# Gated linear attention and a gated projection on one core: scores and values with swapped rows in every second pair, weights in two channel orders, fewer zero products, and a new order of the program

## The chip, the cores and the metric

The kernel runs on one core of a Trainium2 chip. The time is in device microseconds (us), for one execution of the program. The engines are PE (TensorE: matrix products, with PEld for its weight loads), DVE (VectorE), ACT (ScalarE), POOL (GpSimd) and SP (SyncE, which starts the DMAs here). "Clock" is TensorE's granted clock as a share of full speed.

## The reference

```python
f = 1 / (1 + exp(-f_logit))            # B, H, S, D = 4, 8, 768, 48; all float32
for t in range(S):
    state = f[:, :, t, :, None] * state + k[:, :, t, :, None] * v[:, :, t, None, :]
    y[:, :, t] = einsum('bhd,bhde->bhe', q[:, :, t], state)
x = y.transpose(0, 2, 1, 3).reshape(B, S, H * D)           # 4, 768, 384
gate_pre = sum(conv_w[k] * xp[:, k:k + S] for k in range(5))  # causal, per channel
out = (sigmoid(gate_pre) * (x @ w_val)) @ w_out
```

## The kernel before, in words

**Tiles.** The sequence is cut into six blocks `c` of 128 steps. The eight heads go in four pairs `p`; a pair's two heads `s` lie on rows 0 to 47 and 64 to 111 of q, k and the decays. Batches go two by two in halves `h`. Of a block's 128 steps the first 64 and the last 64 are told apart (`u`), since a step looks only at earlier ones.

**Steps of a block.** `csum` (PE, with the triangle `below`; blocks 0 and 1) or `scan` (DVE; blocks 2 to 5) sums the logs of the decays; `pexp`, `pln`, `exp1`, `exp2` on ACT make decays of them; `pmulk` and `pmulq` (DVE) multiply them into k and q. `ktrans` and `kevac` turn k over, `dstate` (PE), `stend` (DVE) and `stmul` (POOL) carry the state `st` from block to block. `scores c b` makes k^T q of a batch on PE, in the four quadrants of 64 rows by 64 columns: per pair two products of 128 columns and two of 64. `mask` (DVE) and `cross` (ACT) bring them to `asb`. `apply c h` makes y^T on PE from the state (part 0) and from `asb` and v (part 1), in columns of 32: head 0's first 32 channels and head 1's are made in two row halves at once ("half height"), the other products with all rows ("full height"). `xevac` (ACT) copies y to `XF`.

**Projections.** `msplit` (ACT) and `mlow` (DVE) split y into a high and a low part. `conv` makes the five taps on PE with diagonal matrices for the blocks in `CONV` (0, 1 and the two halves 5 and 6 of the last block); for blocks 2 to 4 they are made on DVE (`mlast`, `mconv`, 12 per block). `gate` is the sigmoid on ACT, `mval` the product with w_val (nine products of 512 columns for one of three channel groups `m`, 256 columns for a half of the last block), `mmul`, `mhigh`, `mrest` multiply and split again, `mout` is the product with w_out, `mstore` and `out` write it. The conv on PE leaves channel groups in another order of rows (`TURN`) than DVE does, so the gates of blocks 2 to 4 are written in pieces (`MOVES`: 1, 2 and 4 activations for the three groups). The weights come as float64 and are turned into float32 on the chip in `weight` steps (POOL, ACT, DVE).

**Order.** `PROGRAM` is a string of some 500 steps written out in order; `Ordered` chains PE, DVE and ACT to exactly that order. POOL and SP (DMA starts) are ordered by the scheduler from the same string. PSUM is three `pairs` of two banks (`pair`, `done`) and two single banks `mps` (`take`, `give`). `busy n` puts n products with zeros (128x512, bf16) into the bank that the next `pair` or `take` hands out, before its own use. Every fp32 product is two records on PE. Where a decay is out of range a flag sends the program to a general path, which is not run here.

Of the kernel before, what the change touches and what calls it, by code (L numbers as in the profile page):

```python
# [52 lines left out]
ktrans 0 0; exp1 0 1; pmulq 0 1; wload 0; weight 0; weight 0; weight 0; weight 0; pmulq 0 0; busy 3; scores 0 1;
weight 0; mask 0 1; weight 0; weight 0; loadf 1 0; pexp 1 0; loadk 0 2; loadw 0 0; kevac 0 0; dstate 0 0; stend 0 0;
scores 0 0; mask 0 0; pln 1 0; cross 0 1; csum 1 0; exp2 0 2; exp1 0 2; wload 1; pmulk 0 2; ktrans 0 1; cross 0 0;
csum 1 1; okc 0; loadq 0 2; pmulq 0 2; weight 1; weight 1; weight 1; weight 1; weight 1; weight 1; exp2 1 0; loadv 0
0; kevac 0 1; loadw 0 1; dstate 0 1; exp1 1 0; loadv 0 1; apply 0 0 1; stend 0 1; scores 0 3; exp2 1 1; exp1 1 1;
loadk 1 0; pmulk 1 0; ktrans 1 0; weight 1; xevac 0 0; scores 0 2; kevac 1 0; loadk 1 1; pmulk 1 1; ktrans 1 1; weight
2; mask 0 3; cross 0 3; loadq 1 0; pmulq 1 0; busy 2; scores 1 0; weight 2; weight 2; weight 1; weight 3; weight 3;
kevac 1 1; apply 1 0 0; mask 0 2; cross 0 2; scores 1 1; mask 1 0; cross 1 0; loadf 2 0; pexp 2 0; loadv 0 2; apply 0  # L60
1 1; xevac 0 1; weight 2; weight 3; okc 1; weight 2; weight 3; weight 2; weight 3; mask 1 1; cross 1 1; loadq 1 1;
pmulq 1 1; pln 2 0; weight 3; weight 2; loadw 1 0; dstate 1 0; stend 1 0; scores 1 2; mask 1 2; cross 1 2; msplit 0;
scan 2 0; exp2 2 0; exp1 2 0; loadw 1 1; dstate 1 1; stend 1 1; scores 1 3; loadv 1 0; apply 1 0 1; halo 1; xevac 1 0;
conv 0; apply 1 1 0; scan 2 1; exp2 2 1; mask 1 3; weight 3; cross 1 3; mlow 0; wload 2; loadk 2 0; loadk 2 1; pmulk 2
1; ktrans 2 1; loadv 1 1; apply 1 1 1; weight 2; weight 4; stmul 1 1; stmul 1 0; weight 3; mval 0 1; weight 5; weight
4; weight 4; exp1 2 1; okc 2; weight 4; gate 0 0; kevac 2 1; weight 4; weight 4; weight 4; pmulk 2 0; ktrans 2 0;
loadq 2 0; pmulq 2 0; gate 0 1; loadw 2 1; dstate 2 1; weight 5; weight 5; weight 5; gate 0 2; xevac 1 1; mmul 0 1;
# [724 lines left out]
```

## Time and profile before

| | us |
|---|---|
| median of 3 runs (219.23 to 220.79) | 219.87 |
| profiled execution, span from first to last instruction | 217.0 |
| median of the runs above that span | 2.87 |
| PE busy | 196.5 (91%) |
| DVE busy | 147.7 (68%) |
| ACT busy | 140.1 (65%) |

The trace is of one execution. It gives its span; the times of the runs also hold what lies around the span, so a sum over rows is to be compared with 217.0 and not with 219.87. "Busy" is the time in which at least one instruction of the engine runs. PE's count holds products with zeros too.

### The profile page before, as it was taken

The page shows a single profiled execution, that of the slowest core. Times are in us where ns is not written, and L with a number is a line of the kernel's source. Part 1 is how long each engine was busy: PE and PEld are TensorE (multiplying, and loading weights), DVE is VectorE, ACT ScalarE, POOL GpSimd, SP SyncE. Part 2 cuts the span into 40 slices and gives each one's busy share as a digit, 9 for nine tenths or more (in the row PEclk, how much of TensorE's full clock was granted, in tenths as well). Part 3 has the DMA queues.
Part 4 walks back from the last instruction along what each step waited for, and adds up shares of the span by engine and source line. Part 5 has one row for each costly group of instructions (what it writes and reads, how often), then busy time and mean ns, then how long its engine had stood idle before and what let it go on. Part 6 is the DMA issues. An engine that isn't in the chain of part 4 may idle for free.

```text
span 217.0 us, 8352 instructions
## 1 busy us (share of the span) xinstructions
PE 196.5 (91%) x3776; PEld 151.1 (70%) x3778; DVE 147.7 (68%) x200; ACT 140.1 (65%) x220; POOL 33.4 (15%) x43
## 2 busy tenths in 40 slices
PE   3999897939998999999999999999999997989960
PEld 1457786728667876688878878887887885867850
DVE  6005588734999899968789897999686629185000
ACT  4507894436986969778667898787976553645120
POOL 4001205006866323000400002100000000000000
PEclk9999999966999999999999999999999999999996
DMA  6999999977288669262498424012000004100321
GB/s 212 366 377 417 420 425 421 416 276 221 101 316 313 180 239 386 89 189 99 135 309 320 180 91 144 3 51 101 3 5 3 3 0 159 41 0 0 110 108 39
DMA packets 11562, 39.42 MB, mean 182 GB/s; under 512 B 1408, under 2 KB 2304, under 8 KB 10752
## 3 DMA queue, kind: packets, MB, share of 16 engines
q1 hardware_dynamic: 11520, 38.82, 48.8%
q8 instruction: 31, 0.51, 1.0%
q14 instruction: 11, 0.09, 0.1%
HBM read 34.09 MB, written 4.72 MB: 179 GB/s over the span
## 4 chain that ended last, share of the span: by engine, by line
PE 87%; DVE 3%; issue 3%; ACT 2%; DMA 1%; DVEq 0%; ACTq 0%
PE pair L119 60%; PE mps L119 27%; DMA out<-osb 1%; ACT osb L119 1%; DVE keep L119 0%; DVE pair L119 0%; ACT xf L119 0%; DVE e L119 0%; DVE kb L119 0%; ACT qb L119 0%; DVE asb L119 0%; DVE st L119 0%; DVE pre L119 0%; DVE gt L119 0%; ACT e L119 0%
## 5 line engine op out<-in xcount | busy, mean ns | idle before, releaser
L119 ACT ACTIVATE e<-e 112x1024 f32<-112x1024 f32 (+4 forms) x32 | 39.7, 1247 | 4.2 <-DMA e<-in_ft 1.9
L119 PE MATMUL pair<-asb,vb 128*32 128x64 f32 (+2 forms) x1152 | 24.4, 252 | 4.4 <-issue 4.4
L119 DVE SCALAR_TENSOR_TENSOR pre<-xf,cws,pre 128x512 f32<-128x512 f32 x36 | 26.2, 746 | 0.3
L119 PE MATMUL pair<-qb,kb 48*64 48x64 f32 (+1 forms) x768 | 25.0, 260 | 1.3 <-DVE st L119 0.9
L119 PEld LDWEIGHTS pair<-asb,vb 128*32 128x32 f32 (+1 forms) x1152 | 19.5, 111 | 9.2 <-issue 8.5
L119 DVE TENSOR_TENSOR kb<-kb,e 112x1024 f32<-112x1024 f32 (+1 forms) x13 | 16.4, 1272 | 12.9 <-ACT e L119 12.9
L119 DVE TENSOR_TENSOR asb<-pair,tri 128x512 f32<-128x512 f32 x24 | 16.4, 686 | 12.5 <-PE pair L119 12.5
L119 PEld LDWEIGHTS pair<-qb,kb 48*64 48x64 f32 x768 | 21.3, 136 | 4.6 <-DVE st L119 1.0
L119 DVE TENSOR_TENSOR_SCAN e<-keep,e 112x1024 f32<-112x1024 bf16 x8 | 19.1, 2385 | 1.3 <-issue 1.3
L119 PE MATMUL mps<-rg,woH 128*128 128x512 f32 x60 | 19.1, 398 | 0.0
L119 PE MATMUL pair<-idle 128*128 128x512 bf16 x52 | 14.3, 428 | 3.7 <-DVE pair L119 3.6
L119 ACT COPY xf<-pair 128x512 f32<-128x512 f32 (+1 forms) x24 | 10.3, 483 | 11.1 <-PE pair L119 11.1
L119 PE MATMUL mps<-xH,wvH 128*128 128x512 f32 x39 | 16.4, 421 | 0.0
L119 PE MATMUL mps<-xf,WD 32*32 32x256 f32 (+1 forms) x200 | 16.3, 465 | 0.0
L119 ACT ACTIVATE e<-pair 112x1024 f32<-112x1024 f32 (+2 forms) x13 | 9.2, 750 | 11.0 <-PE pair L119 11.0
L119 PE MATMUL pair<-xf,WD 32*32 32x512 f32 (+1 forms) x280 | 15.6, 501 | 0.0
L119 DVE TENSOR_TENSOR qb<-qb,e 112x1024 f32<-112x1024 f32 (+1 forms) x13 | 15.5, 1196 | 0.0
L119 PE MATMUL mps<-xL,wvH 128*128 128x512 f32 x39 | 15.4, 395 | 0.0
L119 PE MATMUL mps<-xH,wvL 128*128 128x512 f32 x39 | 15.4, 395 | 0.0
L119 PE MATMUL pair<-rg,woH 128*128 128x512 f32 (+1 forms) x48 | 12.8, 355 | 2.0 <-ACT osb L119 2.0
L119 ACT COPY asb<-pair 128x256 f32<-128x256 f32 x24 | 8.6, 374 | 8.3 <-DVE asb L119 8.1
L368 POOL TENSOR_TENSOR st<-st,e 112x512 f32<-112x512 f32 x8 | 11.0, 1379 | 17.6 <-ACT ksb L119 9.1
(103 smaller groups left out, 379.8 us busy)
## 6 DMA issues: line engine op xcount, KB each, us to landing
vb<-in_v SPq DMA_DIRECT2D x11, 640.0 KB, 5.9
kb<-in_k SPq DMA_DIRECT2D x11, 512.0 KB, 6.8
qb<-in_q SPq DMA_DIRECT2D x11, 512.0 KB, 7.1
vs<-in_vn SPq DMA_DIRECT2D x10, 512.0 KB, 5.0
e<-in_f SPq DMA_DIRECT2D x4, 1024.0 KB, 6.7
out<-osb SPq DMA_DIRECT2D x15, 256.0 KB, 2.3
raww<-in_wv SPq DMA_DIRECT2D x1, 1152.0 KB, 10.6
raww<-in_wo SPq DMA_DIRECT2D x1, 1152.0 KB, 13.4
```

Of the source, the lines that this page charges most:

```text
L119: ins = emit(*a, **kw)
L368: nc.gpsimd.tensor_tensor(out=s, in0=s, in1=decay(c, h), op=ALU.mult)
```

## The change

- `scores`: odd pairs write their heads to the other row half; pairs 0 and 1 come together, then 2 and 3, first the 128-wide products of both, then the 64-wide ones. The bank is now the pair's parity.
- `apply` has four parts: 0 (state, half height), 1 (state, full height), 2 (values, full height) and 3 (values, half height). v is laid out in 128 columns in place of 160, with both 64-step halves next to each other, and odd pairs with heads swapped.
- `xevac` is one copy in place of two; `gate` of blocks 2 to 4 one activation of 1536 elements in place of seven; two conv banks go in one gate.
- w_val and w_out come in the channel order of the conv on PE (`wvT`, `woT`); the order for blocks 2 to 4 is made from it by `wturn`: two copies on POOL and four DMAs within SBUF (0.79 MB). Weights are loaded in thirds.
- `dstate` takes one bank (`mps`) in place of a pair; four `asb` buffers in place of three; PSUM is one tile `banks`.
- `busy` runs 8 products in all, over the eight banks, in place of 52 (44 ahead of the first `csum`); the three DVE clears of rows 32 to 63 are gone.
- POOL and SP are chained to the program's order too, and `PROGRAM` is written anew.

```diff
-VA, VB = 64, 96
+VA, VB = 64, 64
-MOVES = [[(0, 0, 128)], [(0, 64, 64), (64, 0, 64)], [(r * 32, (r ^ 1) * 32, 32) for r in range(4)]]
+WVB, WVT = 160, 512
+AT = [0, 2 * WVB, WVB]
+LEAD = [0, 64, 32]
 PROGRAM = """
-loadf 0 0; halo 0; pexp 0 0; pln 0 0; busy 44; csum 0 0; loadf 0 1; pexp 0 1; pexp 0 2; pln 0 1; busy 4; csum 0 1; pln
...
+halo 0; loadf 0 0; pexp 0 0; pln 0 0; busy 8; csum 0 0; loadf 0 1; loadv 0 0; loadq 0 0; loadf 1 0; wload 3; loadk 0
...
     PE, DVE, ACT = Ordered(tc, nc.tensor), Ordered(tc, nc.vector), Ordered(tc, nc.scalar)
+    POOL, SP = Ordered(tc, nc.gpsimd), Ordered(tc, nc.sync)
...
-    NA = 3
+    NA = 4
...
     def busy(n):
-        todo[0] = n
...
+        for i in range(n):
+            PE.matmul(banks[:, i % 8], keep[:, 0], keep[:, 0:4], start=True, stop=True)
...
-    for t in pairs:
-        DVE.memset(t[32:64], 0.0)
...
+    def wturn(n):
+        if n == 0:
+            for m in (1, 2):
+                at, k = AT[m], LEAD[m]
+                POOL.tensor_copy(wvT[:, :, :, at + 128 : at + 128 + k], wvT[:, :, :, at : at + k])
+        else:
+            k = LEAD[n]
+            SP.dma_start(woN[: 128 - k, :, n - 1].bitcast(F32), woT[k:, :, n].bitcast(F32))
+            SP.dma_start(woN[128 - k :, :, n - 1].bitcast(F32), woT[:k, :, n].bitcast(F32))
...
     def dstate(c, h):
-        t, ks = pair("d", c, h), KSB[slot(c, h)]
+        t, ks = take("d", c, h), KSB[slot(c, h)]
...
     def scores(c, b):
-        for p in range(NP):
+        for p0 in range(0, NP, 2):
             for u in range(2):
-                for s in range(2):
-                    at = HC * (s ^ u)
-                    PE.matmul(t[at : at + HC, u, p * C : p * C + C - u * HC], kt[rows(s), b * NP + p, u * HC : u * HC + HC],
-                              qt[rows(s), b * NP + p, u * HC :], start=True, stop=True, tile_position=(s * 64, at))
+                for p in (p0, p0 + 1):
+                    for s in range(2):
+                        at, o = HC * (s ^ p & 1), (2 * u + p // 2) * C
+                        PE.matmul(t[at : at + HC, p & 1, o : o + C - u * HC],
+                                  kt[rows(s), b * NP + p, u * HC : u * HC + HC], qt[rows(s), b * NP + p, u * HC :],
+                                  start=True, stop=True, tile_position=(s * 64, at))
...
     def apply(c, h, n):
...
+                    if n == 1:
+                        PE.matmul(to(b, 1, 0, z), st[:, bp, 0:32], qt[:112, bp], start=False, stop=False,
+                                  tile_position=(0, z * 32))
+                    elif n == 2:
+                        PE.matmul(to(b, 1, u, z), vt[:, bp, VA * u : VA * u + 32], at_[:, aat(z, u)],
+                                  start=False, stop=end and c == 0, tile_position=(0, z * 32))
...
+                        for s in range(2):
+                            x = s ^ (z & 1) if n else s
+                            r = slice(x * HC, x * HC + HC)
+                            lhs, rhs = ((vt[r, bp, VA * u + 32 : VA * u + 64], at_[r, aat(z, u)]) if n else
+                                        (st[rows(s), bp, 32:64], qt[rows(s), bp]))
...
-    def mgate(w, m):
+    def mgate(w):
+        act(SIG, w["gt"], w["pre"], AF.Sigmoid)
```

PE at the start. The rows before are the end of the 44 zero products' row and what follows the first `csum` products (`below` is the triangle, `e1` the logs, `ident` the matrix of `ktrans`).

```order
L119 MATMUL pair1_102<-below_72,e10_81 112x128 x4
L119 MATMUL pair2_103<-below_72,e10_81 112x128 x8
L119 LDWEIGHTS idle_80
L119 MATMUL pair0_101<-idle_80 128x512
L119 MATMUL pair0_101<-ident_79,kb0_66 128x112 x8
```

The same place after the change, from the last of the eight zero products on.

```order
L121 MATMUL banks_101<-keep_71 128x512
L121 MATMUL banks_101<-below_72,e10_80 112x128 x16
L121 MATMUL banks_101<-ident_79,kb0_66 128x112 x8
L121 MATMUL banks_101<-below_72,e11_81 112x128 x16
L121 MATMUL banks_101<-ident_79,kb0_66 128x112 x8
L121 MATMUL banks_101<-vs_70,ksb0_87 48x64 x16
L121 MATMUL banks_101<-qb0_64,kb0_66 64x128 x4
```

No zero product stands between the steps any more, and `csum` of block 1 (`e11`) and both `ktrans` of block 0 come ahead of the first scores.

PE in block 2, before: the last pairs of a `scores` (`qb0,kb0`), and the values' part of an `apply` (`asb,vb0`; two batches).

```order
L119 MATMUL pair1_102<-qb0_64,kb0_66 64x128 x2
L119 MATMUL pair1_102<-qb0_64,kb0_66 64x64 x2
L119 MATMUL pair2_103<-asb2_86,vb0_68 32x128 x8
L119 MATMUL pair2_103<-asb0_84,vb0_68 32x128 x8
L119 MATMUL pair2_103<-asb2_86,vb0_68 32x128 x4
L119 MATMUL pair2_103<-asb2_86,vb0_68 32x64 x12
L119 MATMUL pair2_103<-asb0_84,vb0_68 32x128 x4
L119 MATMUL pair2_103<-asb0_84,vb0_68 32x64 x12
```

The same place after: the last pairs of a `scores`, then parts 1, 2 and 3 of an `apply`.

```order
L121 MATMUL banks_101<-qb0_64,kb0_66 64x128 x4
L121 MATMUL banks_101<-qb0_64,kb0_66 64x64 x4
L121 MATMUL banks_101<-qb0_64,st0_74 32x128 x8
L121 MATMUL banks_101<-asb2_85,vb0_68 32x128 x4
L121 MATMUL banks_101<-asb2_85,vb0_68 32x64 x4
L121 MATMUL banks_101<-asb3_86,vb0_68 32x128 x4
L121 MATMUL banks_101<-asb3_86,vb0_68 32x64 x4
L121 MATMUL banks_101<-asb2_85,vb0_68 32x128 x8
L121 MATMUL banks_101<-asb2_85,vb0_68 32x64 x8
L121 MATMUL banks_101<-asb3_86,vb0_68 32x128 x8
L121 MATMUL banks_101<-asb3_86,vb0_68 32x64 x8
```

Of the 64-column products eight a batch are now in the half-height part, and four in the full-height part where twelve stood.

SP's loads, before, from the second load of logs (`in_ft`; `in_vn` is v for `dstate`, `in_wv` w_val).

```order
L645 DMA e11_82<-in_ft 128x1792
L645 DMA kb0_66<-in_k 128x1024
L645 DMA vs_70<-in_vn 128x1024
L221 DMA raww0_94<-in_wv 128x2304
L645 DMA qb0_64<-in_q 128x1024
L645 DMA vb0_68<-in_v 128x640
```

After, from the load that follows the first logs.

```order
L121 DMA vb0_68<-in_v 128x512
L121 DMA qb0_64<-in_q 128x512
L121 DMA e11_81<-in_ft 128x1792
L121 DMA raww0_94<-in_wv 128x768
L121 DMA kb0_66<-in_k 128x512
L121 DMA rawcw_99<-in_cw 128x30
```

The first v, which stood behind the logs of block 1 and all of w_val, now stands ahead of both.

## Rows read from the trace of the kernel before

**Rows 1.** The page, part 1 (busy time, share of the span, instructions of each engine), and from part 2 what the DMA engines moved in 40 equal slices of 5.425 us, in GB/s.

```profile
PE 196.5 (91%) x3776; PEld 151.1 (70%) x3778; DVE 147.7 (68%) x200; ACT 140.1 (65%) x220; POOL 33.4 (15%) x43
GB/s 212 366 377 417 420 425 421 416 276 221 101 316 313 180 239 386 89 189 99 135 309 320 180 91 144 3 51 101 3 5 3 3 0 159 41 0 0 110 108 39
```

**Rows 2.** Busy time of each engine by stretch. Columns: stretch and its length in us, busy us (and instructions) of PE, PEld, DVE, ACT, POOL, granted clock of PE, busy share of the DMA engines (above 1 where transfers overlap), GB/s. 56.78 is the start of block 0's conv on PE, 210.33 the end of the last projection product, 164.70 to 167.43 the conv of a half block.

```profile
0.00:3.65 3.65, 0.00 (x1) 0.10 (x1) 2.19 (x5) 1.39 (x2) 2.42 (x16) 1.00 0.46 135
3.65:15.20 11.55, 11.55 (x44) 4.91 (x44) 1.82 (x2) 4.05 (x9) 0.20 (x1) 1.00 1.02 370
15.20:56.78 41.58, 35.51 (x826) 29.56 (x826) 26.19 (x41) 26.60 (x39) 10.34 (x10) 0.92 0.92 361
56.78:210.33 153.55, 149.30 (x2915) 116.50 (x2908) 117.36 (x152) 107.69 (x170) 20.46 (x17) 1.00 0.36 125
210.33:217.00 6.67, 0.12 (x2) 0.01 (x2) 0.15 (x1) 0.37 (x1) 0.00 (x0) 0.68 0.21 71
60.00:90.00 30.00, 29.19 (x741) 20.63 (x718) 29.04 (x34) 24.32 (x34) 12.70 (x9) 1.00 0.73 261
164.70:167.43 2.73, 2.73 (x122) 2.03 (x121) 2.16 (x3) 1.04 (x2) 0.00 (x0) 1.00 0.02 6
180.00:210.33 30.33, 26.90 (x259) 21.88 (x257) 13.10 (x21) 12.33 (x25) 0.00 (x0) 1.00 0.17 62
```

**Rows 3.** The order in time at the start, PE's rows and two of ACT's. Columns: start in us, us, engine, operation, out<-in, count, and in brackets idle time before it and what ended that.

```profile
3.65 11.77 PE L119 MATMUL pair<-idle 128*128 128x512 bf16 x44 [3.65 <-DVE pair L119]
...
4.25 0.58 ACT L119 ACTIVATE e<-e 128x448 f32<-128x448 f32 x1
...
15.25 1.04 PE L119 MATMUL pair<-below,e 128*112 128x128 f32 x8
...
16.99 2.78 PE L119 MATMUL pair<-below,e 128*112 128x128 f32 x24
```

**Rows 4.** The longest wait of PE in the first 60 us and the stretch behind it, columns as in rows 2.

```profile
43.70:46.20 2.50, 0.02 (x1) 0.00 (x0) 0.00 (x0) 1.03 (x2) 0.00 (x0) 0.86 1.00 379
46.20:52.80 6.60, 5.60 (x118) 5.02 (x120) 3.01 (x5) 3.34 (x5) 1.83 (x3) 0.54 0.65 204
```

**Rows 5.** PE's waits over the span: what was waited for, us in total, times, the longest. "issue" is a wait for which the profile shows no releaser.

```profile
PE pair L119 <- issue: 4.4, 3, 2.5
PE pair L119 <- DVE pair L119: 3.6, 1, 3.6
```

**Rows 6.** PE's order in time from 106 to 116 us: four groups of scores, one `mval`, an `apply` (state, then, after a `ktrans`, values), and the start of a `mout`.

```profile
106.01 3.71 PE L119 MATMUL pair<-qb,kb 48*64 48x128 f32 x128
109.65 0.50 PE L119 MATMUL mps<-xH,wvH 128*128 128x512 f32 x1
...
111.94 1.24 PE L119 MATMUL pair<-qb,st 48*32 48x128 f32 x48
113.11 0.98 PE L119 MATMUL pair<-ident,kb 112*128 112x112 f32 x8
114.03 1.91 PE L119 MATMUL pair<-asb,vb 64*32 64x128 f32 x96
115.87 0.50 PE L119 MATMUL mps<-rg,woH 128*128 128x512 f32 x1
```

**Rows 7.** The values' part of that `apply` in two pieces, columns as in rows 2: half height (both batches), then the full-height part of the first batch.

```profile
114.00:114.60 0.60, 0.60 (x34) 0.40 (x32) 0.60 (x2) 0.57 (x2) 0.00 (x0) 1.00 1.00 396
114.60:115.20 0.60, 0.60 (x40) 0.57 (x36) 0.60 (x2) 0.60 (x1) 0.00 (x0) 1.00 0.92 382
```

**Rows 8.** DVE's instructions in groups by operation and shape. Columns: count, busy us in all, mean ns of one, idle time before them and what ended it.

```profile
L119 DVE SCALAR_TENSOR_TENSOR pre<-xf,cws,pre 128x512 f32<-128x512 f32 x36 | 26.2, 746 | 0.3
L119 DVE TENSOR_TENSOR_SCAN e<-keep,e 112x1024 f32<-112x1024 bf16 x8 | 19.1, 2385 | 1.3 <-issue 1.3
L119 DVE TENSOR_TENSOR asb<-pair,tri 128x512 f32<-128x512 f32 x24 | 16.4, 686 | 12.5 <-PE pair L119 12.5
L119 DVE TENSOR_TENSOR kb<-kb,e 112x1024 f32<-112x1024 f32 x11 | 15.1, 1378 | 0.0
L119 DVE TENSOR_TENSOR qb<-qb,e 112x1024 f32<-112x1024 f32 x11 | 14.2, 1289 | 0.0
L119 DVE TENSOR_TENSOR rg<-gt,rg 128x512 fp32r<-128x512 f32 x15 | 9.9, 683 | 2.1 <-ACT rg L119 2.0
L119 DVE TENSOR_TENSOR xL<-xf,xH 128x1536 fp32r<-128x1536 f32 x5 | 9.0, 1794 | 0.0
L119 DVE TENSOR_TENSOR st<-st,pair 112x512 f32<-112x512 f32 x8 | 5.4, 682 | 4.5 <-PE pair L119 2.8 <-ACT e L119 1.7
L119 DVE SCALAR_TENSOR_TENSOR work<-raww,work 128x384 int32<-128x384 int32 x6 | 4.1, 677 | 0.1
L119 DVE SCALAR_TENSOR_TENSOR work<-work 128x384 int32<-128x384 int32 x6 | 3.3, 550 | 0.1
L119 DVE TENSOR_SCALAR work<-work 128x384 int32<-128x384 int32 x6 | 2.3, 389 | 0.1
```

**Rows 9.** The sigmoids that read `pre` (blocks 2 to 4): count, duration in ns (least, median, most), first and last start in us, shapes.

```profile
L119 ACT ACTIVATE gt<-pre x21: 625/629/634, 127.2 to 196.0; 32x512 f32<-32x512 f32 x12, 64x512 f32<-64x512 f32 x6, 128x512 f32<-128x512 f32 x3
```

**Rows 10.** PE's last products: the end of a group of nine half-width products, and the flag's product behind it.

```profile
209.11 0.40 PE L119 MATMUL pair<-rvb,woH 128*128 128x256 f32 x2
...
210.26 0.19 PE L119 MATMUL mps<-ones,cnt 128*1 128x1 f32 x2
```

More of the change, by code (lines that the diff above doesn't have):

```diff
@@ L53 @@
[L53 to L67, printed above, removed]
@@ L73 @@
-3; pmulk 3 0; mrest 0 0; mrest 0 1; mmul 0 2; mlow 1; pln 4 0; scan 4 0; loadk 4 0; loadk 3 1; exp2 3 1; pmulk 3 1;
-conv 1; apply 2 1 0; ktrans 3 0; kevac 3 0; apply 2 1 1; mval 1 1; loadk 4 1; loadq 3 0; loadw 3 0; dstate 3 0; gate 1
-0; gate 1 1; mmul 1 1; ktrans 3 1; mhigh 0 2; mrest 0 2; xevac 2 1; weight 5; weight 6; halo 3; gate 1 2; scan 4 1;
-mval 1 2; mmul 1 2; exp1 3 1; pmulq 3 1; mlast 2 0; mconv 2 0 0; exp1 3 0; mout 0 2; mstore 0 2; exp2 4 0; mout 0 0;
-mstore 0 0; kevac 3 1; pmulq 3 0; pmulk 4 0; mout 0 1; mhigh 1 2; loadv 4 1; loadq 4 1; loadq 4 0; loadv 4 0; out 0 2;
@@ L78 @@
-dstate 3 1; scores 3 2; stend 3 0; mconv 2 0 1; scores 3 3; stend 3 1; stmul 3 1; mstore 0 1; mhigh 1 1; mask 3 2;
-cross 3 2; mrest 1 1; mlast 2 1; scores 3 0; mask 3 0; scores 3 1; mask 3 1; cross 3 1; mrest 1 2; okc 3; cross 3 0;
-mlast 2 2; exp1 4 0; mval 1 0; mconv 2 1 0; mmul 1 0; mconv 2 1 1; mhigh 1 0; mrest 1 0; apply 3 0 0; out 0 0; ktrans
-4 0; loadv 3 0; apply 3 0 1; mconv 2 2 0; mconv 2 0 2; mconv 2 2 1; mask 3 3; mconv 2 2 2; out 0 1; exp2 4 1; pmulk 4
-1; exp1 4 1; msplit 2; mlow 2; stmul 3 0; loadf 5 0; cross 3 3; mout 1 0; mstore 1 0; xevac 3 0; loadw 4 0; loadk 5 0;
@@ L83 @@
-out 1 0; mconv 2 1 2; mout 1 2; mstore 1 2; mout 1 1; pexp 5 0; mval 2 0; mstore 1 1; mconv 2 0 3; mconv 2 1 3; mconv
-2 2 3; pmulq 4 0; pln 5 0; scan 5 1; kevac 4 0; gate 2 0; gate 2 1; pmulq 4 1; scan 5 0; mval 2 1; mmul 2 1; apply 3 1
-0; ktrans 4 1; loadw 4 1; out 1 2; loadv 3 1; apply 3 1 1; scores 4 1; kevac 4 1; dstate 4 1; xevac 3 1; gate 2 2;
-mhigh 2 1; mlast 3 2; mask 4 1; dstate 4 0; stend 4 0; stend 4 1; mval 2 2; mmul 2 0; mhigh 2 0; okc 4; mmul 2 2;
-cross 4 1; scores 4 0; mask 4 0; cross 4 0; scores 4 2; scores 4 3; mconv 3 2 0; mrest 2 1; mhigh 2 2; mrest 2 2;
@@ new lines @@
+1; conv 1; okc 2; scan 3 1; mask 2 1; weight 5; cross 2 1; mhigh 0 2; msplit 1; exp2 3 1; weight 6; mrest 0 2; mlow 1;
+exp1 3 1; scan 3 0; pmulq 3 1; pmulk 3 1; apply 2 0 1; apply 2 0 2; apply 2 0 3; mval 1 1; gate 1 1; mval 1 0; xevac 2
+0; mlast 2 0; gate 1 0; mlast 2 2; stmul 2 0; weight 6; weight 5; stmul 2 1; halo 2; halo 3; wturn 0; mmul 1 1; mconv
+2 0 0; mconv 2 2 0; mout 0 0; mmul 1 0; mval 1 2; exp2 3 0; exp1 3 0; loadw 3 0; loadq 3 0; pmulk 3 0; pmulq 3 0;
+apply 3 0 0; scores 3 1; loadv 4 0; loadf 4 0; loadv 4 1; loadk 4 0; loadv 3 1; mstore 0 0; out 0 0; loadq 4 0; loadw
@@ new lines @@
+3 1; loadv 3 0; loadq 4 1; loadk 4 1; mlast 2 1; scores 3 0; mconv 2 2 1; mconv 2 0 1; mconv 2 1 0; mout 0 1; mconv 2
+0 2; mmul 1 2; mconv 2 2 2; mout 0 2; msplit 2; pexp 4 0; mask 3 0; mconv 2 1 1; mask 3 1; cross 3 1; ktrans 3 0; pln
+4 0; cross 3 0; ktrans 3 1; mstore 0 1; kevac 3 1; apply 3 0 1; apply 3 0 2; apply 3 0 3; apply 3 1 0; mstore 0 2;
+dstate 3 1; mhigh 1 1; kevac 3 0; dstate 3 0; xevac 3 0; scores 3 2; scores 3 3; scan 4 0; mconv 2 2 3; scan 4 1; mlow
+2; stend 3 0; stend 3 1; mconv 2 1 2; mask 3 3; mconv 2 1 3; mhigh 1 2; mrest 1 2; mask 3 2; exp2 4 1; exp1 4 1; mhigh
@@ L659, in out_ @@
         buf, dst = bufs[n, m]
-        (nc.scalar if engine else nc.sync).dma_start(dst, buf)
+        (ACT if engine else SP).dma_start(dst, buf)
     def mul(n, m):
```

264 lines of the change are left out of this document (139 added, 125 removed).

## The prediction

> **What bounds the kernel now.** I read the page's first part first: PE is busy for 91% of the span, DVE for 68%, ACT for 65% [rows 1]. A kernel at 91% of one engine can gain in only two ways, less work on PE or less time in which PE does something useless or stands, so the second look is at stages [rows 2]. Until 3.65 us PE has nothing. From 3.65 to 15.20 us it is "busy" for 11.55 us with 44 products, and these are the zero products of the step `busy`, queued ahead of the first `csum` [rows 3]: not work. From 15.20 to 56.78 us, where the conv of block 0 starts, it is busy for 35.51 of 41.58 us at a mean clock of 0.92. From there to the last projection product at 210.33 us it is busy for 149.30 of 153.55 us; 6.67 us follow in which only the last store and the flag check run. In the dense middle DVE is as full as PE: 29.04 of 30 us between 60 and 90 us, PE 29.19. After 180 us DVE has 13.1 us of 30, and PE is alone at 26.9. So there are three stages with three limits: A, the start (loads, and what PE waits for); B, up to the last `apply` (PE and DVE together); C, the projections at the end (PE alone).
>
> The profiled execution is the span, 217.0 us, and what the measured time holds around it; the median of the runs, 219.87 us, lies 2.87 us above the span. I sum the span and add 2.87.
>
> **PE work that the change removes.** Scores: four groups take 3.71 us, less the overlap of the last record 3.64, so 0.91 each [rows 6]. Each group has 32 records on four quadrants of the array. Before, two quadrants carry all eight 128-wide ones and the other two the eight 64-wide ones, and 0.91 / 8 = 0.114 us is one 128-wide record on its quadrant (the 24 records of `csum`, each alone on the array, take 2.78 / 24 = 0.116 [rows 3]). A 64-wide one I take from `apply`, whose last batch, 0.58 us of full-height products, holds 2 records of 128 and 6 of 64 columns: (0.58 - 0.23) / 6 = 0.059 [rows 7]. With swapped rows in every second pair each quadrant carries four of either kind: 4 x 0.114 + 4 x 0.059 = 0.69. That is 0.22 less, 5.3 us for 24 groups.
>
> Apply: a half now takes 1.17 us for the state and 1.84 for the values (111.94 to 113.11, 114.03 to 115.87 [rows 6]). The values are 4 x 0.116 of half height, then 4 x 0.116 and 12 x 0.059 of full height, 1.63, and some 0.2 of turning between heights. After: two pieces of 4 x 0.116 + 4 x 0.059 each, 1.40, and one turn less (about 0.15, my reading of the 0.24 that the state's piece has above its eight records). So 0.37 less for each of ten halves, and 0.26 for the two of block 0, which have no state: 4.2 us. Together 9.5 us.
>
> Here a rule of the notes speaks against the change. The trace shows row halves working side by side: both heads of a pair sit on different rows and write one bank in the same group, and that group takes 0.91 us, where its sixteen 128-wide records one after another would take 16 x 0.116 = 1.86 [rows 3, 6]. The Trainium skill, "TensorEngine Tiling (Array Packing)", Gotcha 1: PSUM Pressure, says that different row tiles cannot access the same PSUM bank at once. By that rule the new half-height piece and the swapped scores would run in series; the trace disagrees for partitions that differ, which is how the new pieces write too. I give it a rival below.
>
> **ACT, DVE, POOL.** The gates of blocks 2 to 4 are 21 activations of 0.63 us, 13.2 us [rows 9]; three of 1536 elements replace them. ACT is not full (65%), so this is worth nothing by itself: it unloads the end of B and C. One `xevac` copy for two, one gate for two banks: also ACT only. The three clears of pair rows leave DVE's first 6 us; PE's start waited for the first (3.6 us [rows 5]), but then only zero products began. The two POOL copies and 0.79 MB of weight moves run where POOL has 20 us of 153 and DMA 36% [rows 2]: nothing. `dstate` in one bank instead of a pair and a fourth buffer for the masked scores change no duration; they let PE run further ahead, and I count nothing for that. The zero products, strict order on POOL and SP, and the new program's order are what stage A and the rivals turn on.
>
> **Stage A, to the start of block 0's conv: before 56.78.**
> - Logs ready at 4.25 + 0.58 = 4.83, csum at 15.25, behind 44 zero products [rows 3]. With 8 zero products it starts at about 4.9: -10.4.
> - Three waits of PE for late loads, 4.4 us, the longest of them 2.5 [rows 5], fall if the new load order is right: PE reaches them earlier, but v now comes before f and k of later blocks, in a smaller tile. -4.4.
> - During that longest wait (43.7 to 46.2 us) the granted clock fell to a mean of 0.86, from 46.2 to 52.8 its mean was 0.54, so nearly all of it on the lower of its two levels (1.2 of 2.4 GHz) [rows 4]. 6.6 us at 0.54 cost 6.6 x 0.46 = 3.0. Without the wait they go: -3.0.
> - Six score groups and two applies cheaper: 6 x 0.22 + 2 x 0.26 = -1.8.
> - Two score groups and most of `apply 1 0` stand behind the conv now: -4.3. They are paid in B.
>
> 56.78 - 23.9 = 32.9. This is a lower price, since it has every wait gone. The floor by transfer: in the new order 10.35 MB stand ahead of all that the conv needs of block 1, which the first five slices of the page's rate row (5.425 us each, 9.7 MB) and 1.5 us of the sixth would bring by 28.7 us [rows 1]; then `dstate`, the rest of `apply` and two score groups, 2.4 us: 31. I take 36, which is 32.9 and 3 for waits that a start 10 us nearer to its loads will find, and for a spell at half clock such as [rows 4] shows; bounds 33 (the sum and nothing more) and 42 (the load waits, 4.4, and the half-clock spell, 3, with some 2 for a second one).
>
> The Trainium skill, "TensorE: Matmul & The Clock Gate", HAM oscillation, says that waits for loads between groups of products throw TensorE's clock back to half again and again. By it, 44 zero products dropped would cost what they kept warm. The trace agrees that a wait is followed by half clock [rows 4], in one place; that it happens more often is rival 3.
>
> **Stage B, from there to the last `apply`.** DVE's list by rows [rows 8]: 18 masks x 0.686, 8 scans x 2.385, 8 each of k and q products x 1.378 and 1.289, 24 `mconv` steps x 0.746, 7 `stend` and 11 `mmul` x 0.682, 3 `mlow` x 1.794, 9 `mrest` x 0.683, and 3 each of the weight steps 0.677, 0.550, 0.550, 0.389: 101.0 us. Rows count the end of one instruction under which the next has begun: all DVE rows of that view, of which the largest are shown, add up to 152, and DVE is busy for 147.7 less the clears' 3 [rows 1]. So I take 0.95 of it, 96. PE's work behind A is 149.3 + 4.3 moved in - 7.7 saved (9.5 less the 1.8 in A) = 145.9, of which C holds 51.8 (below), so B has 94 or 95. Two engines at 95 to 96, each waiting for the other: between 60 and 90 us both stood at 97% [rows 2], so 96 / 0.97 = 99, and 3 more since DVE comes out of A with masks and products that A left to it: 102. Bounds 97 (DVE at 99%) and 110 (DVE at 87%).
>
> **Stage C, the projections at the end.** By the order now 13 groups of nine full products remain behind the last `apply`, 2.29 us each (109.65 to 111.94 [rows 6]); 12 half-width groups at 1.1 (209.11 to 210.26 [rows 10]); two half convs at 2.7 [rows 2]; and 3.4 of apply pieces: 51.8. Idle between 180 us and the end was 3.4 us; with DVE at about 25 of 52 I take 2.5: 54. Bounds 51.5 and 57.
>
> **Sum.** 36 + 102 + 54 + 6.67 of tail = 198.7 us of span, and 2.87: 201.5, which I round to **202 us**, 8% faster.
>
> **Rivals.**
> 1. *PE alone sets the time.* A 33, B 97.5, C 52, tail 6.67, 2.87: 192. At the limit 36 + 145.9 + 4.25 idle as before + 6.67 + 2.87 = 195.7. For it: PE at 97% in [rows 2] while DVE was no emptier. Against: PE's list shrinks by 9.5 us, DVE's by nothing, so DVE now decides in B. 191 to 198.
> 2. *The quadrants do not help:* swapped rows or the half-height piece run in series. Half-height 0.70 becomes 1.35: 0.65 x 12 = 7.9 us on PE; the scores' 5.3 stay unpaid. In B part hides behind DVE: 206 to 209. Against it stands the 0.91 above.
> 3. *A slow start.* With 8 zero products PE stands between its first small groups, and the clock is at half for most of A. Ten to twenty us of A's work at half cost 5 to 10 more: 206 to 213. For it: the one wait of 2.5 us in [rows 4] brought 6.6 us of half clock. Against: that spell cost only 3.0, and what it slows is partly waiting for loads anyway.
> 4. *The other side, slower: SP in strict order.* A load that waits for its buffer now holds every later load and store on SP. Place: loads of v and k for blocks 2 to 5, each behind the `apply` or `ktrans` that frees its tile. Price by [rows 4, 5]: 2.5 us of PE standing and 3.0 of half clock, 5.5 each. From 202 it takes four such stalls to pass 222, so it decides from there: 224 to 230 with four or five. Against: DMA is at 36% behind A, so a late load has slack.
> 5. *It does nothing:* 219 to 221, if what the zero products hid was the wait for loads and PE's savings all lie beside DVE. DVE's 29.04 of 30 speaks for the second half, the idle 10.4 us against the first.
>
> **How the numbers follow.** Forecast (198 to 206): 0.52. Rival 1: 0.16. Rival 2: 0.10. Rival 3: 0.16. Rival 4: 0.04. Rival 5: 0.02. The range 195 to 211 takes the forecast, the upper half of rival 1, rival 2 and most of rival 3: about 0.8. A measurement of this kernel tells 1% (2.2 us) from no change: faster 0.94, same 0.02, slower 0.04.
>
> **What would show it.** Stage A: start of the conv of block 0 near 36 us; the first `csum` near 5; granted clock of the first 40 us. Scores: a group of 0.69 us; 1.35 for the half-height piece means rival 2. B: DVE above PE's share between 45 and 130 us. C: 54 us from the last `apply` to the last product. Wrong if the start stays at load-bound 42, if SP shows waits for buffers with PE idle for several us in B, or if DVE's rows grow under contention with POOL's copies.

## The result, and the profile after

The changed kernel takes 212.19 us (median of 5 runs, 211.54 to 218.08) where the kernel before took 219.47 beside it: a ratio of 0.968, interval 0.962 to 0.975. Forecast was 202, range 195 to 211. The direction holds; the size is 40% of the forecast's, and the time lies above the range. Executions of the changed kernel scatter by 2 to 3%, the longer ones mostly at a lower granted clock; the ratios leave these out, while medians and some traces hold them, so the text goes by the ratio and gives the traced execution's time where it matters. The profile shown here is of the same kernel in the first experiment (209.6 us, span 207.8). In the first trace taken (215.55 us) PE stands for "issue" at the same seven places and at two more, 10.6 us in all.

The page: busy time, and the granted clock in 40 slices, first after, then before.

```profile
PE 181.9 (88%) x3732; PEld 148.1 (71%) x3732; DVE 147.5 (71%) x196; ACT 129.2 (62%) x188; POOL 38.0 (18%) x45
PEclk9987996999999988999999969999999999999997
```

```profile
PEclk9999999966999999999999999999999999999996
```

PE's busy time fell by 14.6 us (some 10 of them zero products), the span by 9.2. The stages, columns as in [rows 2]: A to the conv of block 0, B to the last `apply`, C to the last product, the tail, and two stretches inside A.

```profile
0.00:43.53 43.53, 31.80 (x648) 26.75 (x648) 23.80 (x39) 29.45 (x44) 10.36 (x24) 0.92 0.95 353
43.53:156.00 112.47, 104.68 (x2625) 82.54 (x2618) 98.48 (x111) 76.81 (x102) 27.41 (x21) 0.97 0.54 177
156.00:201.30 45.30, 45.30 (x468) 38.85 (x467) 25.07 (x47) 22.56 (x42) 0.22 (x1) 1.00 0.17 62
201.30:207.80 6.50, 0.09 (x2) 0.00 (x0) 0.14 (x1) 0.37 (x1) 0.00 (x0) 0.83 0.21 71
14.00:20.00 6.00, 6.00 (x41) 5.72 (x40) 4.27 (x9) 5.53 (x8) 0.00 (x0) 0.72 1.04 417
28.20:43.53 15.33, 9.51 (x309) 8.01 (x301) 9.27 (x14) 8.62 (x11) 3.00 (x2) 0.89 0.98 348
```

| stage | forecast | measured |
|---|---|---|
| A | 36 | 43.5 |
| B | 102 | 112.5 |
| C | 54 | 45.3 |
| tail | 6.7 | 6.5 |
| around the span | 2.9 | 1.8 |

C is full work and shorter than forecast, A and B are longer. PE's waits (columns as in [rows 5], which held 4.4 us of "issue"):

```profile
PE banks L121 <- issue: 9.1, 7, 2.3
PE banks L121 <- DVE kb L121: 4.0, 2, 3.3
PE banks L121 <- DVE keep L121: 2.3, 1, 2.3
PE banks L121 <- DVE gt L121: 2.2, 1, 2.2
PE banks L121 <- ACT asb L121: 1.5, 3, 0.7
```

Where the long ones lie, in PE's order in time, and the same stretch's full-speed groups of `apply` (parts 1 to 3 of one half, then part 0 of the next) and `scores`:

```profile
13.74 1.50 PE L121 MATMUL banks<-ident,kb 112*128 112x112 f32 x8 [3.26 <-DVE kb L121]
...
30.59 3.81 PE L121 MATMUL banks<-asb,vb 64*32 64x64 f32 x128 [2.31 <-issue]
36.23 0.31 PE L121 MATMUL banks<-asb,vb 128*32 128x64 f32 x6 [1.83 <-issue]
42.33 0.45 PE L121 MATMUL banks<-qb,st 48*32 48x128 f32 x15 [1.67 <-issue]
...
61.75 0.65 PE L121 MATMUL banks<-qb,st 112*32 112x128 f32 x16
62.21 1.83 PE L121 MATMUL banks<-asb,vb 128*32 128x128 f32 x96
63.83 0.74 PE L121 MATMUL banks<-qb,st 48*32 48x128 f32 x32
64.49 1.57 PE L121 MATMUL banks<-qb,kb 48*64 48x128 f32 x64
65.99 0.54 PE L121 MATMUL banks<-vs,ksb 128*48 128x64 f32 x11
...
75.32 0.34 PE L121 MATMUL banks<-qb,kb 48*64 48x64 f32 x6 [2.16 <-issue]
```

The wait of "issue" that ends at 75.32 us stands in the middle of a row of equal products: the 26 records of scores before 73.16 us and the 6 behind 75.32 read the same tiles. A load of v, q or k can hardly be what ends it. What can is PE's own program. The page's part 3 has a queue that loads instructions, and around the last of these waits (72.5 to 75.4 us) it moved one block:

```profile
q8 instruction: 31, 0.51, 1.0%
```

```profile
q8 instruction: 1, 0.02, 2.1%
```

31 blocks of 16 KB, where PE's 3732 products and as many weight loads make 29 times 256 instructions. The waits stand where a block of 256 ends: between the waits that end at 30.59 and 36.23 us lie 128 products with their 128 weight loads, and counted through (with PE's few semaphore instructions) the seven waits of "issue" lie 256, 256, 768, 512, 512 and 2304 instructions apart, whole multiples of 256. Read packet by packet, the blocks begin at 28.31, 33.95, 40.04, 53.26 and 72.95 us, and PE goes on at 30.59, 36.23, 42.33, 55.69 and 75.32: 2.27 to 2.43 us after the block began, each time; the two short waits end 2.37 and 2.14 us after one.

Why PE gets there first can be worked out from the same times. A block's load begins about when PE enters the block before it: behind 143 us, with the DMA engines nearly idle, between 0.4 us earlier and 1.3 us later; for the three blocks that PE waits for up to 42.33 us, with the engines full, 3.4 to 3.9 us later. With the 2.3 us that follow, the next block is there 5.6 to 6.1 us after PE entered the one before, and PE is through that one in 3.8 to 4.4 (30.59 to 34.40 for the 128 products above). With the engines idle it would be there after 3.6 or less.

The kernel before has such waits too. They are the three of [rows 5]:

```profile
34.28 0.38 PE L119 MATMUL pair<-asb,vb 128*32 128x64 f32 x10 [1.13 <-issue]
46.23 1.71 PE L119 MATMUL pair<-asb,vb 128*32 128x64 f32 x46 [2.51 <-issue]
65.95 0.77 PE L119 MATMUL pair<-asb,vb 128*32 128x64 f32 x33 [0.75 <-issue]
```

They lie 511 and 1024 instructions apart, and the blocks that end them begin at 31.93, 43.93 and 63.71 us, 2.24 to 2.35 us earlier. The third lies behind 56.78 us, not in stage A.

### The profile page after: what moved, and what is told of

Same layout as the page of the kernel before. It is cut to its first block, busy times and chain, and to the rows that moved or that the text cites. A ratio compares the mean times of both kernels' runs of the same rounds, so it can differ in the third digit from the quotient of the medians.

```text
span 213.9 us, 8221 instructions
## 1 busy us (share of the span) xinstructions
PE 185.9 (87%) x3732; PEld 151.8 (71%) x3732; DVE 147.2 (69%) x196; ACT 129.5 (61%) x188; POOL 37.3 (17%) x45
## 2 busy tenths in 40 slices
DMA packets 12712, 38.61 MB, mean 181 GB/s; under 512 B 1536, under 2 KB 2944, under 8 KB 12160
## 4 chain that ended last, share of the span: by engine, by line
PE 63%; DVE 16%; issue 7%; ACT 5%; DMA 4%; SPq 2%; DVEq 0%; ACTq 0%
PE banks L121 63%; DMA kb<-in_k 4%; DVE e L121 4%; DVE pre L121 3%; DVE kb L121 3%; SPq L121 2%; ACT e L121 2%; DVE asb L121 2%; DVE qb L121 1%; DVE gt L121 1%; ACT asb L121 1%; DVE st L121 1%; ACT gt L121 1%; DVE rg L121 1%; ACT xH L121 1%
## 5 line engine op out<-in xcount | busy, mean ns | idle before, releaser
L121 PE MATMUL banks<-xH,wvT 128*128 128x512 f32 x90 | 33.0, 431 | 2.9 <-DVE gt L121 2.2
L121 PE MATMUL banks<-asb,vb 64*32 64x64 f32 (+3 forms) x1152 | 23.6, 253 | 4.5 <-issue 4.4
L121 PEld LDWEIGHTS banks<-asb,vb 64*32 64x32 f32 (+1 forms) x1152 | 20.8, 110 | 6.7 <-issue 5.2
L121 PE MATMUL banks<-rg,woT 128*128 128x512 f32 (+1 forms) x108 | 24.7, 370 | 1.0 <-DVE gt L121 1.0
L121 PE MATMUL banks<-qb,kb 48*64 48x64 f32 (+1 forms) x768 | 22.4, 263 | 2.4 <-issue 2.4
L121 DVE TENSOR_TENSOR asb<-banks,tri 128x512 f32<-128x512 f32 x24 | 16.1, 684 | 11.6 <-PE banks L121 11.5
L121 PEld LDWEIGHTS banks<-xH,wvT 128*128 128x128 f32 x90 | 18.4, 204 | 7.9 <-DVE gt L121 2.4
L121 PEld LDWEIGHTS banks<-qb,kb 48*64 48x64 f32 x768 | 19.8, 144 | 5.4 <-issue 4.8
L121 PEld LDWEIGHTS banks<-rg,woT 128*128 128x128 f32 x108 | 18.0, 188 | 4.7 <-DVE gt L121 1.5
L121 PE MATMUL banks<-xL,wvT 128*128 128x512 f32 x45 | 18.9, 421 | 0.0
L121 ACT COPY osb<-banks 128x512 f32<-128x512 f32 x15 | 8.8, 587 | 10.4 <-PE banks L121 7.2
```

The costliest lines, as they stand in the source:

```text
L121: ins = emit(*a, **kw)
```

## The experiments

Theory F: PE stands because its next block of instructions has not arrived. Theory V: it stands for late loads of v, as the prediction had read the same waits. The kernel before had medians of 218.2 to 219.3 us beside them.

**1. The kernel once more, and its blocks moved.** Products of one column behind the zero products move every later block by 16 to 192 instructions. They change nothing else but PE's start, where they add up to 1.1 us (the wait for k's products ends at 13.7 to 14.9 us in place of 13.74).

```diff
+    def tiny(n):
+        for i in range(n):
+            PE.matmul(banks[:, i % 8, 0:1], keep[:, 0], keep[:, 0, 0:1], start=True, stop=True)
...
-busy 8; csum 0 0;
+busy 8; tiny 32; csum 0 0;
```

> The changed kernel once more, timed beside the others. 211 to 213 us. Theory F (PE stands because its next 16 KB of instructions have not arrived): the trace has 8 to 10 waits of PE without a releaser ("issue"), 9 to 12 us in all, at the same steps as before: in apply of block 0 (twice, 2 us), in the scores of block 2 (1.9 us), in dstate of block 4 (1.9 us). Theory V (late loads of v, as the prediction had read them): the same.

> The changed kernel with 32 products of one column behind the 8 zero products: 64 more instructions on PE, so that every later 16 KB load of PE's instructions begins 64 instructions earlier in the program; about 1 us of work. Theory F: the issue waits move to other steps, or change length by over 1 us where they stay; each ends 2.3 to 2.8 us after a 16 KB load began; their sum is between 4 and 13 us, and the time goes 1 to 4 us either way from 212. Theory V: the same four steps wait 1.9 to 2.1 us each; 212 to 213.5 us.

> As the run with 64 more instructions, with 64 products of one column and so 128 more instructions. Theory F: again other steps, another sum of waits (4 to 13 us), 207 to 216 us. Theory V: the same steps and lengths, 212.5 to 214.5 us.

> As the run with 64 more instructions, with 96 products of one column and so 192 more instructions. Theory F: again other steps, 207 to 217 us. Theory V: the same steps and lengths, 213 to 215.5 us.

> The changed kernel with 8 products of one column behind the zero products, 16 more instructions on PE. Theory F: the waits stay near the same steps but each is 0.1 to 0.6 us longer or shorter; 209 to 215 us. Theory V: 211 to 212.

Measured: 211.28 us for the kernel once more, ratio 0.968 (0.959 to 0.976); with 64 instructions more 216.38, 0.988 (0.980 to 0.997); with 128 214.35, 0.976 (0.968 to 0.985); with 192 212.53, 0.968 (0.960 to 0.976). With 16 more the four executions took 213.3 to 220.2 us, too far apart for a ratio. The longest wait of each, with 64, 128 and 192 more:

```profile
35.16 1.71 PE L121 MATMUL banks<-asb,vb 128*32 128x64 f32 x38 [3.93 <-issue]
```

```profile
46.18 6.71 PE L121 MATMUL banks<-xf,WD 32*32 32x512 f32 x104 [4.01 <-issue]
```

```profile
44.12 0.91 PE L121 MATMUL banks<-qb,kb 48*64 48x128 f32 x15 [4.17 <-issue]
```

The second stands inside the conv of block 0, behind 16 of its records, which read nothing but y and a constant. The waits sum to 12.1, 10.1, 12.1 and 10.7 us (64, 128, 192 and 16 more; the traced executions took 216.7, 215.8, 215.7 and 213.3 us). In all four traces they stand on the same grid of 256 instructions, and so, with 64, 128 and 192 more, at other steps. So does, to within two records, every wait of "issue" of over 0.5 us in all the traces of this case but one (the gates' run in 4). Theory V falls; F holds. Two of F's sizes were missed: with 64 more the time rose by over 4 us, and with 16 more the first two waits changed from 2.31 and 1.83 to 0.38 and 3.46 us, where 0.1 to 0.6 was expected. Why 192 more cost nothing by the ratio isn't shown; the traced execution was the longest of its four.

**2. Data traffic taken away.** In the first, q, k and v of blocks 2 to 5 are cut to one pair per load; in the second those of blocks 1 to 5 and w_out (the rest is zero or old). Outputs are then not the reference's.

```diff
     def load(dst, src, c, x0, x1):
+        if c >= 2 and src is not f:
+            dst, x1 = dst[:, 0:1], x0 + 1
```

> The changed kernel with the loads of q, k and v of blocks 2 to 5 cut to one pair of the four or eight that they bring (an eighth to a quarter of their bytes; the blocks then use old values, all instructions stay). Theory F with traffic (an instruction load starts late, and PE stands, because data loads stand ahead of it on the DMA engines): behind the first 30 us the 16 KB loads start within 0.5 us of the instruction that stands 256 before, the issue waits fall from 9 or 10 us to 4 or less, the granted clock goes over 0.97, 200 to 206 us. Theory F without traffic (instruction loads are late by themselves): issue waits stay at 8 us or more, 208 to 212 us.

> The changed kernel with nearly all data traffic taken away: of q, k and v of blocks 1 to 5 and of w_out only a small part is loaded (the rest is zero or old), all instructions on PE, DVE and ACT stay, two clears on DVE and three on POOL come at the start. The logs, block 0 and w_val are loaded as before. Theory F with traffic: the 16 KB loads of PE's instructions start within 1 us of their place, the issue waits of the first 45 us fall from 5.8 us to 2.5 or less, the conv of block 0 starts at 34 to 39 us (the prediction's 36), the time is 198 to 204 us. If instruction loads are late by themselves or the start is bound by the order of work: conv at 41 us or later, 206 to 212 us.

Measured: 208.43 us, ratio 0.944 (0.935 to 0.953), issue waits 7.0 us where F with traffic had forecast 4 or less. The second took 208.01 us, ratio 0.937 (0.928 to 0.947); its trace is of the longest of four executions (204.7 to 209.6 us):

```profile
PE banks L121 <- DVE gt L121: 5.5, 3, 2.8
PE banks L121 <- DVE kb L121: 4.6, 2, 3.8
PE banks L121 <- issue: 4.2, 3, 3.4
```

```profile
34.67 0.31 PE L121 MATMUL banks<-asb,vb 128*32 128x64 f32 x6 [3.38 <-issue]
41.55 4.94 PE L121 MATMUL banks<-xf,WD 32*32 32x512 f32 x120
```

Traffic is part of the cause: behind 45 us, where hardly any is left, the issue waits are 0.8 us in place of 3.3, and the one long wait that remains stands while a megabyte of logs goes by (27.8 to 32.7 us). But the conv starts at 41.55, not at 34 to 39, the waits of the first 45 us are 3.4 us and not 2.5 or less, and the time is not 198 to 204. Without the 3.38 us it would start at about 38.2, an estimate; what is left is the wait for k's products (3.8 us, behind the logs) and the half clock that follows it (0.72 from 14 to 20 us). The shorter start also turns into waits for the gates (5.5 us in place of 2.2). So traffic is shown to delay the blocks; that it is the whole of the lost start is not.

**3. Loads held back.** A small ACT copy holds SP's row back until the conv of block 0: w_out, k and v of block 2 in the first; k and q first and a third of w_out not held in the second; the hold one step earlier in the third.

```diff
+    def hold():
+        ACT.copy(RAW["wo"][:, 0:1, 0].bitcast(F32), ones)
...
-loadf 2 0; wload 6; loadk 2 0; loadv 2 0; loadv 1 1;
+loadf 2 0; loadv 1 1;
...
-cross 1 3;
+cross 1 3; hold; wload 6; loadk 2 0; loadv 2 0;
```

> The changed kernel with a small ACT copy behind the last cross of block 1 that holds the loads of w_out and of k and v of block 2 back until the conv of block 0 begins; v of block 1 goes ahead of them. Between 31 and 42 us the DMA engines then have little to do. Theory F with traffic: the third and fourth 16 KB loads of PE's instructions start within 1.5 us of their place in place of 2.3 to 3.2, the two issue waits near 34 and 41 us (3.5 us together) fall to 1 us or less, the conv of block 0 starts 2 to 4 us earlier (40 to 41.5 us); the time is 208 to 211 us, if block 2 isn't late in turn. Without traffic as the cause: these waits stay, conv at 43 to 45 us, 211 to 214 us.

> As the run that holds loads back behind the last cross of block 1, but the first third of w_out is not held, and k and q of block 2 come first behind the hold, v and the rest of w_out after. Theory F with traffic: the conv of block 0 starts at 40 to 41.5 us again in place of 43.5, the granted clock of the first 45 us is over 0.93. If what the first form lost (ACT's gate 2.8 us behind the weight steps, v of block 2 1.5 us late) came from these two loads: 208 to 211 us. If block 2's loads are late in any order: 213 to 216.

> As the run before, with the hold one step earlier (behind cross 1 2, about 1.5 us), so that k of block 2 comes 1.5 us sooner and meets the fourth 16 KB load of PE's instructions. Theory F with traffic: of the gain in the start 1 to 2 us are lost again (conv at 41 to 43 us). 208.5 to 212 us.

Measured: 215.75 us, ratio 0.984 (0.979 to 0.988); 217.46 (213.6 to 219.05, no ratio; the trace is of 217.9 us); 215.13, 0.988 (0.977 to 0.998), its executions from 210.85, the traced one, to 217.25. The first:

```profile
35.10 0.31 PE L63 MATMUL banks<-asb,vb 128*32 128x64 f32 x6 [0.26 <-issue]
40.44 4.94 PE L63 MATMUL banks<-xf,WD 32*32 32x512 f32 x120
50.94 1.98 PE L63 MATMUL banks<-qb,kb 48*64 48x128 f32 x64 [2.81 <-ACT gt L63]
64.12 1.85 PE L63 MATMUL banks<-asb,vb 128*32 128x128 f32 x96 [1.46 <-DMA vb<-in_v]
```

The start does what F says (40.4 us), and block 2 gives it back: the gate stands on ACT behind weight steps that wait for w_out, and v is late. In the second form the conv starts at 44.45 us, not at 40 to 41.5, and waits of 2.67 and 2.77 us appear where the held loads now run; in the third at 41.4. Traffic moved is waits moved. None is faster than the changed kernel (0.968), and the first is slower, where 208 to 211 us was expected.

**4. One part undone.** Old quadrants of the scores; old form of the values' 64-column products; gates in 21 pieces; POOL and SP free; 44 zero products back (with 84 of one column, 256 instructions in all). The first two compute other values. The diffs show the main lines.

```diff
-        for p0 in range(0, NP, 2):
+        for p in range(NP):
             for u in range(2):
...
-                        at, o = HC * (s ^ p & 1), (2 * u + p // 2) * C
...
+                    at = HC * (s ^ u)
...
```

```diff
+                    elif n == 3 and u == 1:
+                        for g in (0, 2):
+                            PE.matmul(to(b, g, 1, z), vt[:, bp, VA + 32 : VA + 64], at_[:, aat(z, 1)],
...
```

```diff
-        act(SIG, w["gt"], w["pre"], AF.Sigmoid)
+        for m in range(NM):
+            for z in range(0, 128, (128, 64, 32)[m]):
+                n = (128, 64, 32)[m]
+                act(SIG, w["gt"][z : z + n, m], w["pre"][z : z + n, m], AF.Sigmoid)
```

```diff
-    POOL, SP = Ordered(tc, nc.gpsimd), Ordered(tc, nc.sync)
+    POOL, SP = nc.gpsimd, nc.sync
```

```diff
-busy 8; csum 0 0;
+busy 52; tiny 84; csum 0 0;
```

> The changed kernel with the scores' products in the old quadrants and the old order (the same head on the same row half in every pair; which pair's values meet which is then wrong, sizes are the same). A group takes 0.91 us again in place of 0.75, 24 x 0.16 = 3.9 us of PE. If PE's work sets the time: 215 to 216 us. Theory F: slower groups give the instruction loads time, the issue waits fall by 1 to 3 us, and the time rises by 0 to 2.5 us: 211.5 to 214.

> The changed kernel with apply's 64-column products of head parts in the old form (full height, three in a row per pair; which steps meet is then wrong, the number and sizes of products are the old ones). 0.25 to 0.35 us more of PE for each of 12 halves, 3 to 4 us. If PE's work sets the time: 214.5 to 215.5. Theory F: the slower products give the instruction loads time, issue waits fall by 1 to 3 us, 211 to 213.5 us.

> The changed kernel with the gates of blocks 2 to 4 as 21 activations of 512 columns again in place of three of 1536; 13 us of ACT in place of 4 to 5. ACT has slack: within 1.5 us of the changed kernel, 210 to 213 us. If ACT is what B waits for: 215 us or more.

> The changed kernel with POOL and SP ordered by the scheduler again in place of strictly by the program. If strict order on SP holds loads back (rival 4): 2 us or more faster, 206 to 209 us. If not: within 1.5 us of 211 to 212.

> The changed kernel with 52 zero products in place of 8 ahead of the first csum, and 84 products of one column, so that PE has exactly 256 instructions (16 KB) more and the later loads of instructions begin at the same steps. About 10 us of zero products and 2 us of small ones. If the start is work in a row: the conv of block 0 starts 9 to 12 us later and the time is 221 to 224 us. Theory F and loads: 3 to 7 us later, since the waits for k (3.3 us) and a part of the issue waits go: 214 to 218 us. Rival 3 (zero products keep the clock): the granted clock of the first 45 us goes over 0.97 and the time is within 2 us of 211.

| undone | us | ratio to before | slower than the changed kernel, by the ratios, us |
|---|---|---|---|
| nothing (a0) | 211.28 | 0.968 (0.959 to 0.976) | |
| scores | 211.78 | 0.966 (0.957 to 0.975) | -0.4 |
| apply | 214.66 | 0.984 (0.977 to 0.992) | 3.6 |
| gates | 219.11 | 0.998 (0.994 to 1.003) | 6.8 |
| strict order on POOL, SP | 214.30 | 0.978 (0.972 to 0.985) | 2.4 |
| few zero products | 218.14 | 0.990 (0.980 to 0.999) | 4.8 |

By the two intervals, each difference is known to 2 to 3 us either way, so -0.4 can't be told from nothing, and 2.4 hardly.

Scores: two old groups take 1.89 us (65.46 to 67.35) in place of 1.50, 0.2 more for each of 24, nearly 5 us of PE. By the ratios the time does not rise; the traced span is 209.6 us in place of 207.8, and the issue waits fall from 9.1 us:

```profile
PE banks L121 <- issue: 6.5, 6, 2.9
```

So at least half of that gain, 2.6 us in the traces, went where F says. Apply's 3.6 us came through, where F had forecast 211 to 213.5 us; its issue waits are 8.8 us, hardly less than 9.1. With free queues the issue waits are 13.0 us. The gates were the surprise. In the changed kernel, and undone:

```profile
116.76 1.48 ACT L121 ACTIVATE gt<-pre 128x1536 f32<-128x1536 f32 x1
...
118.27 0.69 DVE L121 TENSOR_TENSOR gt<-banks,gt 128x512 f32<-128x512 f32 x1 [2.53 <-ACT gt L121]
...
119.02 0.50 PE L121 MATMUL banks<-xH,wvT 128*128 128x512 f32 x1 [2.23 <-DVE gt L121]
```

```profile
119.13 4.34 ACT L121 ACTIVATE gt<-pre 128x512 f32<-128x512 f32 x7
123.50 0.69 DVE L121 TENSOR_TENSOR gt<-banks,gt 128x512 f32<-128x512 f32 x1 [5.38 <-ACT gt L121]
124.24 0.79 PE L121 MATMUL banks<-xH,wvT 128*128 128x512 f32 x1 [5.09 <-DVE gt L121]
...
168.10 2.78 PE L121 MATMUL banks<-xf,WD 32*32 32x256 f32 x120 [1.29 <-issue]
```

PE waits for a bank, the bank for `mmul` on DVE, DVE for the gate. The gate itself is 4.34 - 1.48 = 2.9 us longer in each of three blocks, but PE stands for it longer in block 2 alone (5.09 in place of 2.23). In block 3 it stands 1.29 us up to 168.10; that is put down to "issue" but lies 16 instructions off the grid of 256, just behind the `mmul` that waited 3.04 us for its gate and ended at 167.90. In block 4 it doesn't stand at all. That is some 4.2 of the 6.8 us; where the rest goes isn't shown. ACT is at 62%, and still the gate is in the chain.

**5. One part alone, in the kernel before.** 36 of the 44 zero products cut to one column; and one activation per channel group for each gate (rows then not in their order).

```diff
-        for _ in range(todo[0]):
-            PE.matmul(t, idle[:, 0:128], idle[:], start=True, stop=True)
+        for i in range(todo[0]):
+            w = 1 if todo[0] == 44 and i >= 8 else B * C
+            PE.matmul(t[:, 0:w], idle[:, 0:128], idle[:, 0:w], start=True, stop=True)
```

```diff
-            for a, z, n in MOVES[m]:
+            for a, z, n in MOVES[0]:
```

> The kernel before with 8 of its 44 first zero products as they were and 36 cut to one column (the same number of instructions, so the 16 KB loads of instructions begin at the same steps); 9 us of zero products less. The prediction's term: 9 us faster, 210 to 211 us. Rival 3 (without zero products PE's clock is at half in the start): 215 to 219 us, with a granted clock under 0.8 in the first 45 us. Theory F: between, 212 to 216, since the loads of k and the instruction loads come no earlier.

> The kernel before with one activation for each channel group's gate in blocks 2 to 4 (9 in place of 21, rows then not put back in their order; 7.5 us less on ACT). If the gates stand in the chain in any order: 2 to 4 us faster, 215 to 217 us. If they matter only in the new order, where all three groups' gates stand in one place ahead of the products: within 1 us of 219.

Measured: 216.33 us, ratio 0.988 (0.979 to 0.996); and 219.38, 1.004 (1.000 to 1.008). Dropping 36 zero products gives 2.7 us (by the interval 1 to 5), not 9: `csum` starts 7 us earlier, and the gain meets the same instruction block and a wait for a bank:

```profile
40.84 0.98 PE L119 MATMUL pair<-asb,vb 128*32 128x64 f32 x46 [2.51 <-issue]
45.30 1.95 PE L119 MATMUL pair<-vs,ksb 128*48 128x64 f32 x32 [3.48 <-ACT xf L119]
```

The clock of the first 45 us is 0.97, where it was 1.00 and rival 3 wanted under 0.8, and that of the whole run 0.974 (before, beside it, 0.975 to 0.995), so the zero products did little to keep it. The gates are worth nothing in the old order, where each group's gate had its own place.

## Why the prediction was wrong

**Stages.** A, B and C were the right cut, and C alone PE's (45.30 of 45.30 us).

**Stage A, the late loads: the step that failed.** "Three waits of PE for late loads, 4.4 us ... fall if the new load order is right." They were blocks of PE's own instructions, and one of the three (0.75 us) was not in stage A. The new load order did not take them away: in the changed kernel A holds three of them, 5.8 us (2.31 + 1.83 + 1.67) in place of 3.6. That PE's small products now follow one another more closely fits this, but no run shows it by itself. With the 3.26 us for k's products, which the sum did not see behind the zero products, and a clock of 0.92 (3.5 us of 43.5), that is 12.6 us against an allowance of 3.1 over 32.9; some 2 us came in better elsewhere. The term of -10.4 for the zero products was nearly right as a start time (5.65 us, forecast 4.9) and wrong as a gain: alone it brought 2.7.

**The clock.** It was to be free of half speed once no wait was left. Each of the four longest waits is still followed by it: 0.72 between 14 and 20 us, behind the 3.26 us, and lower slices near 31, 76 and 120 us, behind those of 2.31, 2.16 and 2.23. Rival 3's range (206 to 213) holds the measured time, but not by its mechanism: the clock of A is 0.92, not half for most of it. With 44 zero products back the clock of the first 45 us was 0.96 against 0.92, and yet the conv started 9.0 us later (52.57) and the time was 4.8 us longer.

**Scores and apply.** Scores: 0.75 where 0.69 was worked out (64.49 to 65.99 for two). Apply: 2.74 a half (0.66 part 0, 0.46 part 1, 1.62 parts 2 and 3) where 2.64 was; 0.27 less than before, not 0.37. The mechanism held, and rival 2 fell: row halves that write one bank at other partitions still run side by side, sixteen 128-wide records and sixteen 64-wide ones in 0.75 us, where the first alone would take 1.86 one after another. The rule of the Trainium skill, "TensorEngine Tiling (Array Packing)", Gotcha 1: PSUM Pressure, fell with it for this case. But only apply's part clearly reached the end; that half or more of the scores' 4 us would come back as shorter waits was not in the sum.

**The gates.** "Worth nothing by itself" is true in the old order (ratio 1.004) and 6.8 us off, give or take 2, in the new one. The step looked at ACT's share, 65%, and not at who waits for the gate.

**B and C together** came out at 157.8 us against 156, by errors that cancel. In C, a group of nine products back to back takes 2.10 us (193.76 to 195.86), not 2.29, which holds the start behind small products: 2.5 us; no idle time: 2.5; the 3.4 of apply pieces ended in B. In B, instruction waits (3.3 us) and clock (3% of 112) made up the rest. DVE was at 98.5 of 112.5 us, where 96 of 102 were forecast. That DVE would set the pace in B did not hold: PE was busy for 104.7 us there, not 94 or 95, and between 45 and 130 us for 78.3 of 85 us where DVE was for 75.4.

```profile
193.76 0.86 PE L121 MATMUL banks<-rg,woT 128*128 128x512 f32 x3
194.46 1.56 PE L121 MATMUL banks<-rg,woN 128*128 128x512 f32 x6
195.86 0.86 PE L121 MATMUL banks<-rg,woT 128*128 128x512 f32 x3
```

**Around the span.** 2.87 us set a median of other runs beside one span. Run by run it is 1.7 to 1.8 us (209.6 and 207.8 here; 217.73 and 216.0 for the kernel before).

**Rival 4** fell: strict order on SP and POOL is no loss; without it the kernel was 2.4 us slower, hardly clear of noise.

**Open.** The parts undone one by one sum to more than the whole gain (-0.4 + 3.6 + 6.8 + 2.4 + 4.8 = 17.2 of 7.1 us): each is priced in an order made for it, and what the new order is worth with the old parts was not run. By what way data traffic makes a block's load begin up to 3.9 us after PE entered the block before isn't shown.
